# Fourier folds on one engine, half of their first level early, and other products between the folds and the DFT

## The chip, the core and the metric

The kernel runs on one core of a Trainium2 chip. The core has five engines that each work through a queue of their own in order: TensorE (PE in the profile, its weight loads PEld), VectorE (DVE), ScalarE (ACT), GpSimd (POOL) and SyncE (SP, which here only starts transfers). TensorE writes its products to eight PSUM banks; the other engines take them from there to SBUF. The metric is the device time of one execution in microseconds, the median of several runs.

## The reference

Two blocks follow each other, in float32. The first is a decayed linear attention over 4 batches, 8 heads, 768 positions and head size 64. Its output, as x of 4 x 768 x 512, goes through a Fourier mix, a normalisation and an MLP:

```
X = np.fft.fft(x, axis=1)
X = np.fft.fft(X, axis=2)
u = x + np.real(X)
un = (u - mean(u)) / sqrt(var(u) + 1e-6)
out = u + maximum(un @ w_ch1, 0) @ w_ch2        # w_ch1: 512 x 2048, w_ch2: 2048 x 512
```

The weights come as 64-bit floats, so the kernel turns them into float32 itself.

## The kernel before

**Stages of one batch.** `attn_chunk(b, c)` computes 128 of the 768 positions of batch b, for c from 0 to 5: transposes of k and q, scores, state, output and a last transpose into the tile x (for c of 3 and above: xn), which stays in SBUF and is also written to a tensor in DRAM, `xd[b]`. `fft_ln(b)` does the Fourier transform by symmetry. `mirror(b)` gathers rows of `xd[b]` in reversed order with indirect transfers that GpSimd issues: two tiles r0 and r1 (L339) and three tiles x (L342). `fold(b, r1)` adds and subtracts rows and columns that mirror each other, in two blocks of 128 and 65 rows (`BLK`). The even parts (tile e, L358, L359, L362, L368, L369, L375, L376) are VectorE's; the odd ones (tile o, L360, L361, L364, L371, L372, L378, L379) are GpSimd's. The results f and f1 (tag fs, fq) are the stationary operands of the sequence DFT (L395, five groups i, each over both blocks). `width` does the transform over columns (L406 to L411), lines 429 to 433 add the result to x, and three groups g of two tiles are normalised and transposed (L450 to L466). `mlp(b)` then goes through the three groups: 16 products with w1 (L477), whose results ScalarE and VectorE clip in turn (L483, L485), and two tiles T with 16 products with w2 each (L491), which VectorE adds to u and which are written out.

**Units of weights.** `weights()` converts the weights in 32 units (16 of w1, 16 of w2), each five instructions on VectorE (L216 to L224) and three on ScalarE.

**Order.** The kernel is written as generators that yield an estimate, in microseconds, of the TensorE work that they have just emitted. `weave(lead, other, ratio)` emits a step of `lead` and then steps of `other` until their sum is `ratio` times that of `lead`. When `other` runs out, the rest of `lead` is emitted in one go. The framework then fixes each engine's queue ahead of time: in the order of emission where the inputs are expected to be there, with later work moved ahead of what is expected to wait. At run time nothing overtakes.

- Batch 0's attention runs with 12 units of weights. Its `fft_ln(0)` runs beside half of batch 1's attention and 4 units.
- The rest of batch 1's attention and the start of `fft_ln(1)` run beside `mlp(0)` and the last 16 units.
- For batches 2 and 3, `front(b + 1)` (attention, then `fft_ln`) runs beside `mlp(b)` at the ratio 0.9 * t_mlp / t_front, 0.9 * 163.2 / 60.8 = 2.42.

**Rings.** Tiles of one tag share a ring of buffers. PSUM has a ring pa of five banks (attention, DFT, normalisation) and a ring pm of three (MLP). The tiles x come from a ring of ten, six of which a batch holds until its MLP tile T has been written.

Of the kernel before, what the change touches and what calls it, by code (L numbers as in the profile page):

```python
# [20 lines left out]
def _consts(B, S, DM):  # L21
# [38 lines left out]
    rows = [S // 2 - p, np.maximum(S // 2 - 128 - p, 0)]  # L60
    rev = [S - 128 * t - p for t in range(S // 256)]
    rows += [r % S for r in rev]
# [11 lines left out]
def kernel(  # L74
# [60 lines left out]
    z = fp.tile([H, 2 * C], F32, tag="fo", name="z")  # L135
# [28 lines left out]
    shifted = fp.tile([C, H, C], F32, tag="fe", name="shifted")  # L164
# [76 lines left out]
    def attn_chunk(b, c):  # L241
# [76 lines left out]
        if c == 0:  # L318
            xd[b] = dram.tile([S, DM], F32, name=f"xd{b}")
        nc.scalar.dma_start(xd[b][rows], x)  # L320
# [12 lines left out]
    def mirror(b):  # L333

        d = xd[b]
        gather = nc.gpsimd.indirect_dma_start
        r1 = [new(fp, [128, DM], f"r{a}") for a in range(2)]
        for a, n in enumerate(BLK):
            gather(out=r1[a][0:n], out_offset=None, in_=d[:, :], in_offset=row_of(a, n))  # L339
        for t in range(HC):  # L340
            u = xs[b, HC + t] = new(xp, [128, DM], "x")
            gather(out=u[:, :], out_offset=None, in_=d[:, :], in_offset=row_of(2 + t))  # L342
        for t in range(HC):
            xs[b, t] = xn_.pop((b, t))
        return r1

    def fold(b, r1):

        sets, odd = [], []
        for a, n in enumerate(BLK):  # L350
            x0, x2, x3 = xs[b, a][0:n], xn_[b, HC + a][0:n], xs[b, HC + a][0:n]
            x1 = r1[a][0:n]

            e, o = new(fp, [128, 2, 2 * W], "fe"), new(fp, [128, 2, 2 * W], "fo")
            f = new(fp, [128, 4, 2, QM], "fs", bufs=2)
            f1 = new(fp, [128, 2, 1], "fq", bufs=2)
            V, P = nc.vector, nc.gpsimd
            V.tensor_tensor(e[0:n, 0, 0:DM], x0, x3, op=ALU.add)  # L358
            V.tensor_tensor(e[0:n, 1, 0:DM], x1, x2, op=ALU.add)  # L359
            P.tensor_tensor(o[0:n, 0, 0:DM], x0, x3, op=ALU.subtract)  # L360
            P.tensor_tensor(o[0:n, 1, 0:DM], x1, x2, op=ALU.subtract)  # L361
            V.tensor_tensor(e[0:n, :, 1:HM], e[0:n, :, 1:HM], e[0:n, :, HM:DM - 1], op=ALU.add)  # L362
            nc.scalar.copy(e[0:n, :, HM:HM + 1], e[0:n, :, DM - 1:DM])
            P.tensor_tensor(o[0:n, :, 1:HM], o[0:n, :, 1:HM], o[0:n, :, HM:DM - 1], op=ALU.subtract)  # L364
# [19 lines left out]
    def fft_ln(b):  # L384
# [31 lines left out]
        def halves(t):  # L416
            return t.rearrange("p (r k) -> p r k", r=2)
# [170 lines left out]
```

## Time and profile before

| | |
|---|---|
| median of three runs | 1000.22 us (999.79 to 1003.56) |
| the profiled execution | 1007.08 us, its span 1005.3 us |
| mean granted TensorE clock | 0.937 of 2.4 GHz |
| TensorE busy | 892.6 us |
| VectorE, ScalarE, GpSimd busy | 323.7, 186.1 and 165.7 us |

All times inside the profile are of that one execution, from its first instruction. "Idle before" an instruction is the time in which its engine did nothing, put down to the event that ended it. The granted clock is a share of 2.4 GHz; 0.50 is 1.2 GHz.

### The profile page before, as it was taken

What the parts mean: (1) busy time and instruction counts of PE and PEld (TensorE: products, weight loads), DVE (VectorE), ACT (ScalarE), POOL (GpSimd) and SP (SyncE); (2) the same over time, 40 slices, a digit from 0 to 9 for tenths busy, and PEclk for the clock granted to TensorE, in tenths of its full rate; (3) what the DMA queues carried; (4) which work ended last, traced back from release to release, by engine and by line L of the source; (5) the groups of instructions that cost most, each with busy time, mean ns of one, the idle gap of its engine ahead of it and who ended that gap; (6) DMA issues with size and microseconds to landing.
All of it is one profiled execution on the core that took longest, in us unless ns stands there. A gap on an engine that the chain in (4) does not pass through costs nothing.

```text
span 1005.3 us, 10721 instructions
## 1 busy us (share of the span) xinstructions
PE 892.6 (89%) x4404; PEld 616.0 (61%) x4404; DVE 323.7 (32%) x610; ACT 186.1 (19%) x411; POOL 165.7 (16%) x176
## 2 busy tenths in 40 slices
PE   4642989598899999999986999999986999999997
PEld 3531867445575848658645848658646847576673
DVE  5978389833510101111124511111124411000100
ACT  4662247411010101111101101111101100000000
POOL 2219130413200001000034201000034200000000
PEclk9985799786999999999996999999995999999999
DMA  9982258400000002122120002121020000000000
GB/s 253 252 221 68 64 154 233 143 5 16 22 1 22 0 11 53 42 70 58 42 78 11 1 12 53 43 60 46 11 69 11 1 11 11 11 10 1 22 0 22
DMA packets 89265, 55.59 MB, mean 55 GB/s; under 512 B 76764, under 2 KB 78308, under 8 KB 89216
## 3 DMA queue, kind: packets, MB, share of 16 engines
q1 hardware_dynamic: 83264, 40.73, 15.5%
q0 software_dynamic: 2496, 7.87, 2.4%
q10 hardware_dynamic: 3456, 6.29, 1.7%
q8 instruction: 35, 0.57, 0.2%
q14 instruction: 14, 0.11, 0.0%
HBM read 42.29 MB, written 12.59 MB: 55 GB/s over the span
## 4 chain that ended last, share of the span: by engine, by line
PE 73%; POOL 6%; DVE 6%; issue 3%; DMA 3%; ACT 1%; POOLq 0%; ACTq 0%
PE pm L477 30%; PE pm L491 29%; PE pa L395 4%; PE pa L306 2%; PE pa L274 2%; DMA x<-xd,ix 1%; PE pa L302 1%; PE pa L465 1%; PE pa L313 1%; PE pa L289 1%; POOL fo L360 1%; POOL fo L364 1%; POOL r L339 1%; DVE pw L219 1%; PE pa L261 1%
## 5 line engine op out<-in xcount | busy, mean ns | idle before, releaser
L477 PE MATMUL pm<-ut,w 128*128 128x256 f32 x1536 | 356.9, 389 | 1.7 <-DVE hr L483 0.7
L491 PE MATMUL pm<-w,hr 128*128 128x512 f32 x768 | 338.5, 594 | 0.0
L477 PEld LDWEIGHTS pm<-ut,w 128*128 128x128 f32 x1536 | 293.3, 194 | 47.7 <-issue 5.4
L491 PEld LDWEIGHTS pm<-w,hr 128*128 128x128 f32 x768 | 143.3, 191 | 163.2 <-issue 162.2
L483 DVE TENSOR_SCALAR hr<-pm 128x256 f32<-128x256 f32 x96 | 40.6, 423 | 236.9 <-PE pm L477 236.9
L485 ACT ACTIVATE hr<-pm 128x256 f32<-128x256 f32 x96 | 36.6, 383 | 384.1 <-PE pm L477 379.9
L395 PE MATMUL pa<-cs,fs 65*128 65x193 f32 (+1 forms) x128 | 42.7, 509 | 63.8 <-DVE fs L375 49.6
L497 DVE TENSOR_TENSOR y<-pm,x 128x256 f32<-128x256 f32 x24 | 10.2, 424 | 218.6 <-PE pm L491 218.6
L395 PEld LDWEIGHTS pa<-cs,fs 65*128 65x128 f32 (+1 forms) x128 | 36.2, 309 | 70.1 <-issue 39.4
L502 POOL DMA_INDIRECT out_dram<-y,ix x12 | 12.5, 1043 | 325.2 <-DVE y L498 324.9
L252 POOL TENSOR_TENSOR kd<-k,decay 128x512 f32<-128x512 f32 x20 | 22.4, 1119 | 229.4 <-issue 136.1
L274 PE MATMUL pa<-qT,kT 64*128 64x128 f32 x384 | 30.5, 298 | 11.4 <-ACT qT L263 11.4
L278 DVE TENSOR_TENSOR sc<-pa,decay 128x512 f32<-128x512 f32 x48 | 31.3, 684 | 22.0 <-PE pa L274 20.3
L274 PEld LDWEIGHTS pa<-qT,kT 64*128 64x128 f32 x384 | 25.4, 199 | 21.0 <-ACT qT L263 14.1
L306 PE MATMUL pa<-sc,v 128*64 128x128 f32 x384 | 31.0, 291 | 5.7 <-DVE sc L278 5.7
L266 DVE TENSOR_TENSOR qs<-pa,qpow 128x512 f32<-128x512 f32 x20 | 13.8, 689 | 64.5 <-ACT qT L263 64.5
L306 PEld LDWEIGHTS pa<-sc,v 128*64 128x64 f32 x384 | 23.2, 143 | 12.6 <-DVE sc L278 8.2
L433 POOL TENSOR_TENSOR x<-x,ds 128x512 f32<-128x512 f32 x12 | 18.2, 1515 | 77.3 <-DVE ds L430 70.4
L339 POOL DMA_INDIRECT r<-xd,ix x8 | 8.6, 1079 | 129.4 <-DMA xd<-xn 128.2
L258 ACT COPY kT<-pa 128x512 f32<-128x512 f32 x24 | 14.1, 589 | 76.7 <-PE pa L256 76.6
L217 ACT ACTIVATE pw<-pw,cvt 128x512 uint16<-128x512 uint16 x32 | 22.9, 720 | 26.0 <-DVE pw L216 25.8
L309 ACT COPY oT<-pa 128x512 f32<-128x512 f32 x24 | 14.0, 585 | 65.0 <-PE pa L306 65.0
(94 smaller groups left out, 714.1 us busy)
## 6 DMA issues: line engine op xcount, KB each, us to landing
raw<-in_moe_w_ch_dram SPq DMA_DIRECT2D x32, 512.0 KB, 5.5
k<-in_k_dram SPq DMA_DIRECT2D x24, 256.0 KB, 3.3
q<-in_q_dram SPq DMA_DIRECT2D x24, 256.0 KB, 4.1
v<-in_v_dram SPq DMA_DIRECT2D x24, 256.0 KB, 3.4
xd<-x ACTq DMA_DIRECT2D x12, 256.0 KB, 2.7
xd<-xn ACTq DMA_DIRECT2D x12, 256.0 KB, 2.1
out_dram<-y SPq DMA_DIRECT2D x12, 256.0 KB, 2.0
cs<-k_cs SPq DMA_DIRECT2D x1, 772.0 KB, 6.9
```

Source lines behind the costliest of these rows:

```text
L217: nc.scalar.activation(pw, pw, AF.Relu, bias=cvt[:, 0:1], scale=-1.0)
L252: nc.gpsimd.tensor_tensor(kd, kt, kpow, op=ALU.mult)
L274: mm(pss[hi][:, hp, :], lhsT=kT[HD[hi], hp, :], rhs=qT[HD[hi], hp, :], start=True, stop=True)
L278: nc.vector.tensor_tensor(t, pss[hi], decay[:, hi::2, :], op=ALU.mult)
L306: mm(po[HD[hi], hp, :], lhsT=vt[:, 2 * hp + hi, :], rhs=sc[hi][:, hp, :], start=(c == 0 and hp == 0), stop=(hp == HP - 1), skip_group_chec ...
L339: gather(out=r1[a][0:n], out_offset=None, in_=d[:, :], in_offset=row_of(a, n))
L395: nc.tensor.matmul(ps[0:m, n, :], lhsT=f, rhs=cs[0:rows, a, i in (2, 3), n, :], start=(a == 0), stop=(a == 1))
L433: nc.gpsimd.tensor_tensor(halves(v_), halves(v_), halves(ds[:, 1:DM + 1])[:, ::-1, :], op=ALU.add)
L477: nc.tensor.matmul(ps, lhsT=w1[:, c, 128 * fc:128 * fc + 128], rhs=ut[:, c, :], start=(c == 0), stop=(c == KO - 1))
L483: nc.vector.tensor_scalar(t, ps, 0.0, None, op0=ALU.max)
L485: nc.scalar.activation(t, ps, AF.Relu)
L491: nc.tensor.matmul(ps, lhsT=hr[fc // 4][:, fc % 4, 128 * i:128 * i + 128], rhs=w2[:, fc, :], start=(fc == 0), stop=(fc == FO - 1))
```

## The change

1. All folds are VectorE's. Results overwrite parts of e and o instead of going to f and f1, and DFT groups read them there through `piece`.
2. `xd[b]` becomes two tensors: one for positions 128 to 639, one for 512 to 767 and row 0. Chunk 4 is written to both; of chunk 0 only one row is written.
3. `mirror_a(b)` is emitted at the end of chunk 4: it gathers r0, r1 and one tile x and does half of the first level of both blocks (`fold_x` with i = 1). `fold(b)`, after chunk 5, gathers the other two tiles x and does the rest. Tiles e and o now exist twice (fe0, fe1, fo0, fo1). What was one instruction on both halves of a block (L362, L364) is now one on each half.
4. `fft_ln` yields 7.0 after the folds, and 1.0 ahead of the transposes of each group g. t_front becomes 70.7, so that the ratio of batches 2 and 3 becomes 2.08.
5. For batch 0, `next(mix)` emits the folds. Then 0.3 t_att of batch 1's attention (two chunks) and two units of weights are emitted, then the DFT beside two further chunks and four units.
6. The addition of line 433 goes from GpSimd to VectorE.

```
@@ -57,9 +57,11 @@
     p = np.arange(128)
-    rows = [S // 2 - p, np.maximum(S // 2 - 128 - p, 0)]
+    ha, hb = S - 256, 128 * (S // 256) + 128
     rev = [S - 128 * t - p for t in range(S // 256)]
-    rows += [r % S for r in rev]
+    rows = [S // 2 - 128 - p, np.maximum(S // 2 - 256 - p, 0)]
+    rows += [r - hb for r in rev[:2]] + [r - 128 for r in rev[2:]]
     for b in range(B):
         rows += [S * b + np.where(r == S, S // 2, r) for r in rev]
     ix = np.ascontiguousarray(np.stack(rows, axis=1)).astype(np.uint32)
...
@@ -316,8 +318,14 @@
         nc.scalar.copy(x[:, 0:HM], px[:, 0:HM])
         nc.scalar.copy(x[:, HM:DM], px[:, DM - 1:HM - 1:-1])
         if c == 0:
-            xd[b] = dram.tile([S, DM], F32, name=f"xd{b}")
-        nc.scalar.dma_start(xd[b][rows], x)
+            xd[b] = (dram.tile([S - 256, DM], F32, name=f"xa{b}"), dram.tile([257, DM], F32, name=f"xb{b}"))
+            nc.scalar.dma_start(xd[b][1][256:257], x[0:1])
+        elif c < NC - 1:
+            nc.scalar.dma_start(xd[b][0][(c - 1) * C:c * C], x)
+        if c >= NC - 2:
+            nc.scalar.dma_start(xd[b][1][(c - NC + 2) * C:(c - NC + 3) * C], x)
+        if c == NC - 2:
+            mirror_a(b)
         yield 1.7
...
@@ -330,60 +338,73 @@
     for t in ys + bs:
         nc.gpsimd.memset(t, 0.0)
-    def mirror(b):
-        d = xd[b]
-        gather = nc.gpsimd.indirect_dma_start
+    gather = nc.gpsimd.indirect_dma_start
+    eo = {}
+    def fold_x(b, a, n, i, lo, hi):
+        e, o = eo[b][a]
+        tt = nc.vector.tensor_tensor
+        tt(e[0:n, i, 0:DM], lo, hi, op=ALU.add)
+        tt(o[0:n, i, 0:DM], lo, hi, op=ALU.subtract)
+        tt(e[0:n, i, 1:HM], e[0:n, i, 1:HM], e[0:n, i, HM:DM - 1], op=ALU.add)
+        tt(o[0:n, i, 1:HM], o[0:n, i, 1:HM], o[0:n, i, HM:DM - 1], op=ALU.subtract)
+    def mirror_a(b):
+        xa = xd[b][0]
         r1 = [new(fp, [128, DM], f"r{a}") for a in range(2)]
+        eo[b] = [(new(fp, [128, 2, 2 * W], f"fe{a}"), new(fp, [128, 2, 2 * W], f"fo{a}")) for a in range(2)]
         for a, n in enumerate(BLK):
-            gather(out=r1[a][0:n], out_offset=None, in_=d[:, :], in_offset=row_of(a, n))
-        for t in range(HC):
+            gather(out=r1[a][0:n], out_offset=None, in_=xa[:, :], in_offset=row_of(a, n))
+        for t in range(2, HC):
             u = xs[b, HC + t] = new(xp, [128, DM], "x")
-            gather(out=u[:, :], out_offset=None, in_=d[:, :], in_offset=row_of(2 + t))
+            gather(out=u[:, :], out_offset=None, in_=xa[:, :], in_offset=row_of(2 + t))
+        for a, n in enumerate(BLK):
+            fold_x(b, a, n, 1, r1[a][0:n], xn_[b, HC + a][0:n])
+    def fold(b):
+        for t in range(2):
+            u = xs[b, HC + t] = new(xp, [128, DM], "x")
+            gather(out=u[:, :], out_offset=None, in_=xd[b][1][:, :], in_offset=row_of(2 + t))
         for t in range(HC):
             xs[b, t] = xn_.pop((b, t))
-        return r1
-    def fold(b, r1):
-        sets, odd = [], []
+        sets = []
+        tt = nc.vector.tensor_tensor
         for a, n in enumerate(BLK):
-            x0, x2, x3 = xs[b, a][0:n], xn_[b, HC + a][0:n], xs[b, HC + a][0:n]
-            x1 = r1[a][0:n]
-            e, o = new(fp, [128, 2, 2 * W], "fe"), new(fp, [128, 2, 2 * W], "fo")
-            f = new(fp, [128, 4, 2, QM], "fs", bufs=2)
-            f1 = new(fp, [128, 2, 1], "fq", bufs=2)
-            V, P = nc.vector, nc.gpsimd
-            V.tensor_tensor(e[0:n, 0, 0:DM], x0, x3, op=ALU.add)
-            V.tensor_tensor(e[0:n, 1, 0:DM], x1, x2, op=ALU.add)
-            P.tensor_tensor(o[0:n, 0, 0:DM], x0, x3, op=ALU.subtract)
-            P.tensor_tensor(o[0:n, 1, 0:DM], x1, x2, op=ALU.subtract)
-            V.tensor_tensor(e[0:n, :, 1:HM], e[0:n, :, 1:HM], e[0:n, :, HM:DM - 1], op=ALU.add)
+            fold_x(b, a, n, 0, xs[b, a][0:n], xs[b, HC + a][0:n])
+            e, o = eo[b][a]
             nc.scalar.copy(e[0:n, :, HM:HM + 1], e[0:n, :, DM - 1:DM])
-            P.tensor_tensor(o[0:n, :, 1:HM], o[0:n, :, 1:HM], o[0:n, :, HM:DM - 1], op=ALU.subtract)
             am, bm = e[0:n, :, W:2 * W], o[0:n, :, W:2 * W]
             lo, hi = e[0:n, 0, 0:HM + 1], e[0:n, 1, 0:HM + 1]
-            V.tensor_tensor(am[:, 0, 0:HM + 1], lo, hi, op=ALU.add)
-            V.tensor_tensor(am[:, 1, 0:HM + 1], lo, hi, op=ALU.subtract)
+            tt(am[:, 0, 0:HM + 1], lo, hi, op=ALU.add)
+            tt(am[:, 1, 0:HM + 1], lo, hi, op=ALU.subtract)
+            lo, hi = am[:, :, 0:QM], am[:, :, HM:QM:-1]
+            tt(e[0:n, :, 0:QM], lo, hi, op=ALU.add)
+            tt(e[0:n, :, QM:HM], lo, hi, op=ALU.subtract)
             lo, hi = o[0:n, 0, 1:HM], o[0:n, 1, 1:HM]
-            P.tensor_tensor(bm[:, 0, 1:HM], lo, hi, op=ALU.subtract)
-            P.tensor_tensor(bm[:, 1, 1:HM], lo, hi, op=ALU.add)
-            lo, hi = am[:, :, 0:QM], am[:, :, HM:QM:-1]
-            V.tensor_tensor(f[0:n, 0], lo, hi, op=ALU.add)
-            V.tensor_tensor(f[0:n, 1], lo, hi, op=ALU.subtract)
+            tt(bm[:, 0, 1:HM], lo, hi, op=ALU.subtract)
+            tt(bm[:, 1, 1:HM], lo, hi, op=ALU.add)
             lo, hi = bm[:, :, 1:QM + 1], bm[:, :, HM - 1:QM - 1:-1]
-            P.tensor_tensor(f[0:n, 2], lo, hi, op=ALU.subtract)
-            P.tensor_tensor(f[0:n, 3], lo, hi, op=ALU.add)
-            nc.scalar.copy(f1[0:n], am[:, :, QM:QM + 1])
-            sets.append((f, f1))
-        return sets
+            tt(o[0:n, :, 0:QM], lo, hi, op=ALU.subtract)
+            tt(o[0:n, :, QM:HM], lo, hi, op=ALU.add)
+            sets.append((e, o))
+        eo.pop(b)
+        def piece(a, i, n):
+            c0 = W + QM if i == 4 else QM * (i % 2)
+            return sets[a][i in (2, 3)][0:BLK[a], n, c0:c0 + (1 if i == 4 else QM)]
+        return piece
     def fft_ln(b):
-        r1 = mirror(b)
-        sets = fold(b, r1)
+        piece = fold(b)
+        yield 7.0
         for i in range(5):
...
@@ -391,8 +412,7 @@
             m = 128 if i < 4 else 1
             for n in range(2):
                 for a, rows in enumerate(BLK):
-                    f = sets[a][0][0:rows, i, n, :] if i < 4 else sets[a][1][0:rows, n, :]
-                    nc.tensor.matmul(ps[0:m, n, :], lhsT=f, rhs=cs[0:rows, a, i in (2, 3), n, :],
+                    nc.tensor.matmul(ps[0:m, n, :], lhsT=piece(a, i, n), rhs=cs[0:rows, a, i in (2, 3), n, :],
                                      start=(a == 0), stop=(a == 1))
             nc.scalar.copy(ys[i][0:m, 0:2 * NK].rearrange("p (k n) -> p n k", n=2), ps[0:m])
             yield 1.4
...
@@ -430,7 +450,7 @@
             nc.vector.tensor_tensor(even_odd(ds[:, HM + 1:2 * HM + 1]), A, even_odd(B[:, :]), op=ALU.add)
             u, v_ = xs[b, t], xs[b, HC + t]
             nc.vector.tensor_tensor(halves(u), halves(u), halves(ds)[:, :, 0:HM], op=ALU.add)
-            nc.gpsimd.tensor_tensor(halves(v_), halves(v_), halves(ds[:, 1:DM + 1])[:, ::-1, :], op=ALU.add)
+            nc.vector.tensor_tensor(halves(v_), halves(v_), halves(ds[:, 1:DM + 1])[:, ::-1, :], op=ALU.add)
             yield 1.6
             if t == 0:
                 ps = psum_a([128, DM])
...
@@ -453,6 +473,7 @@
             rs = new(np_, [128, G], "rs")
             nc.gpsimd.tensor_scalar(ve, mv[:, :, 1], EPS, None, op0=ALU.add)
             nc.gpsimd.tensor_tensor(rs, ve, mhalf, op=ALU.pow)
+            yield 1.0
             ut = uts[b, g] = new(np_, [128, KO, G * 128], "ut")
             for i in range(G):
                 un = new(np_, [128, DM], "un", bufs=1)
...
@@ -540,16 +561,19 @@
     NW = KO * DFF // WP
     w = weights()
     t_mlp = NG * (FO * 1.7 + G * 4 * 3.4)
-    t_att, t_front = NC * 7.3, NC * 7.3 + 17.0
+    t_att, t_front = NC * 7.3, NC * 7.3 + 7.0 + 7.0 + 5.7 + 3 * 2.4
     run(weave(attn(0), part(w, 0.75 * NW), 0.75 * NW / t_att))
     fr = front(1)
-    run(weave(fft_ln(0), weave(part(fr, 0.5 * t_att), part(w, 0.25 * NW), 0.5 * NW / t_att), 1.5))
+    mix = fft_ln(0)
+    next(mix)
+    run(weave(part(fr, 0.3 * t_att), w, 0.1))
+    run(weave(mix, weave(part(fr, 0.3 * t_att), part(w, 0.25 * NW), 1.0), 1.0))
     for b in range(B):
         back = mlp(b)
         if b == 0:
-            run(weave(part(fr, 0.5 * t_att), weave(part(back, FO * 1.7 - 1.0), w, 0.9), 1.0))
+            run(weave(part(fr, 0.4 * t_att), weave(part(back, FO * 1.7 - 1.0), w, 0.9), 1.0))
             run(w)
             run(weave(fr, back, 1.0))
         elif b + 1 < B:
```

## Rows read from the trace of the kernel before

**Rows 1.** The page: busy us, share of the span and instructions of each engine.

```profile
PE 892.6 (89%) x4404; PEld 616.0 (61%) x4404; DVE 323.7 (32%) x610; ACT 186.1 (19%) x411; POOL 165.7 (16%) x176
```

**Rows 2.** Waits of PE, whole span: us in total, times, longest.

```profile
PE pa L395 <- DVE fs L375: 49.6, 4, 27.1
PE pa L395 <- POOL fs L378: 14.1, 3, 4.8
```

**Rows 3.** Busy us (instructions) by stretch: PE, PEld, DVE, ACT, POOL; PEclk, DMA, GB/s.

```profile
19.70:65.00 45.30, 30.41 (x400) 24.50 (x400) 42.05 (x70) 29.53 (x55) 10.04 (x10) 1.00 0.98 265
65.00:92.06 27.06, 0.01 (x2) 0.03 (x1) 18.87 (x22) 6.82 (x13) 16.65 (x15) 0.58 0.39 108
92.06:113.40 21.34, 17.95 (x85) 15.20 (x86) 10.71 (x16) 4.88 (x10) 9.26 (x7) 0.50 0.12 28
136.90:209.20 72.30, 56.43 (x366) 45.30 (x367) 63.03 (x118) 41.80 (x77) 18.39 (x18) 0.83 0.59 176
203.20:208.00 4.80, 4.49 (x11) 3.64 (x12) 4.80 (x10) 1.99 (x4) 0.00 (x0) 0.50 0.00 0
234.70:249.90 15.20, 15.15 (x50) 11.80 (x51) 1.39 (x4) 3.00 (x8) 1.17 (x2) 0.50 0.00 0
271.60:513.60 242.00, 242.00 (x1157) 163.79 (x1157) 32.49 (x69) 27.90 (x64) 10.70 (x12) 1.00 0.13 33
530.70:543.70 13.00, 8.17 (x22) 6.73 (x23) 8.91 (x9) 1.16 (x4) 9.56 (x9) 0.50 0.01 1
756.70:775.40 18.70, 13.82 (x39) 12.38 (x40) 8.95 (x10) 2.16 (x6) 9.61 (x9) 0.50 0.00 0
```

**Rows 4.** The same of line 224 alone, once for each weight unit: DVE busy.

```profile
136.90:209.20 72.30, 11.53 (x15) 0.83 0.59 176
```

**Rows 5.** Timeline around the third batch's fold: start, us, engine, line [idle before].

```profile
512.97 0.60 PE L313 MATMUL pa<-ident,oT 128*128 128x128 f32 x4
...
514.28 0.33 ACTq L320 DMA_DIRECT2D xd<-xn  x1
...
520.62 0.69 DVE L359 TENSOR_TENSOR fe<-r,xn 128x512 f32<-128x512 f32 x1 [15.80 <-DMA r<-xd,ix]
...
523.04 3.42 DVE L358 TENSOR_TENSOR fe<-x,x 128x512 f32<-128x512 f32 x1 [1.06 <-DMA x<-xd,ix]
523.40 1.28 POOL L361 TENSOR_TENSOR fo<-r,xn 128x512 f32<-128x512 f32 x1
...
530.71 2.52 PE L395 MATMUL pa<-cs,fs 128*128 128x193 f32 x6 [6.39 <-DVE fs L375]
...
539.76 2.30 PE L395 MATMUL pa<-cs,fs 65*128 65x193 f32 x6 [4.82 <-POOL fs L378]
```

**Rows 6.** Timeline around the first batch's fold.

```profile
65.72 0.33 ACTq L320 DMA_DIRECT2D xd<-xn  x1
...
77.35 0.69 DVE L359 TENSOR_TENSOR fe<-r,xn 128x512 f32<-128x512 f32 x1 [6.90 <-DMA r<-xd,ix]
...
92.06 0.98 PE L395 MATMUL pa<-cs,fs 128*128 128x193 f32 x2 [27.05 <-DVE fs L375]
...
98.24 0.41 DVE L369 TENSOR_TENSOR fe<-fe 65x257 f32<-65x257 f32 x1
```

**Rows 7.** Groups of instructions by line, shapes apart: busy, mean ns, idle before.

```profile
L358 DVE TENSOR_TENSOR fe<-x,x 128x512 f32<-128x512 f32 x4 | 10.7, 2687 | 4.3 <-DMA x<-xd,ix 4.3
...
L433 POOL TENSOR_TENSOR x<-x,ds 128x512 f32<-128x512 f32 x12 | 18.2, 1515 | 77.3 <-DVE ds L430 70.4 <-ACT ds L428 3.4 <-DMA x<-xd,ix 2.5
```

**Rows 8.** Waits of VectorE for a gather, whole span.

```profile
DVE fe L359 <- DMA r<-xd,ix: 37.7, 3, 15.8
```

**Rows 9.** Timeline around the second batch's late gather.

```profile
224.62 0.41 DVE L498 TENSOR_TENSOR y<-pm,x 128x256 f32<-128x256 f32 x1
...
225.31 0.98 POOL L342 DMA_INDIRECT x<-xd,ix  x1 [22.48 <-DVE y L498]
...
228.62 0.69 DVE L358 TENSOR_TENSOR fe<-x,x 65x512 f32<-65x512 f32 x1 [3.59 <-DMA x<-xd,ix]
```

More of the change, by code (lines that the diff above doesn't have):

```diff
@@ L130, in psum_m @@
         return new(pm, shape, "pm")
-    z = fp.tile([H, 2 * C], F32, tag="fo", name="z")
+    z = fp.tile([H, 2 * C], F32, tag="fo0", name="z")
     sq = const.tile([H, 8], F32, name="sq")
@@ L163 @@
     nc.vector.tensor_copy(flip, ident[:, ::-1])
-    shifted = fp.tile([C, H, C], F32, tag="fe", name="shifted")
+    shifted = fp.tile([C, H, C], F32, tag="fe0", name="shifted")
     nc.sync.dma_start(shifted, bass.AP(z0.tensor, z0.offset, [[1, C], [2 * C, H], [1, C]]))
```

## The prediction

> **What bounds the kernel now.** I read busy times first [rows 1]: TensorE works 892.6 of 1005.3 us, the others a third of the span or less. The kernel is bound by TensorE where TensorE is fed, as in the 242 us stretch without any idle time at full clock in [rows 3]. What can be won lies in the rest, so the waits of TensorE came next [rows 2]. Two of them, both of the DFT (L395) for the folds, make 49.6 + 14.1 = 63.7 us. Then I asked the stretches behind these waits for their granted clock [rows 3]: each of the four folds leaves TensorE at 0.50, that is at 1.2 instead of 2.4 GHz, for some time after work has resumed. Half of the busy time there is lost: 17.95/2 = 9.0 us behind batch 0's fold, (4.49 + 15.15)/2 = 9.8 behind batch 1's, 8.17/2 = 4.1 behind batch 2's and 13.82/2 = 6.9 behind batch 3's, together 29.8. All that the folds cost is so 63.7 + 29.8 = 93.5 us. More cannot be won by curing them alone.
>
> Last I read the timeline around a fold [rows 5] to see what the wait is made of. Batch 2: the last transpose ends at 513.57, and the first fold has its gathered rows at 520.62. That is 7.05 us for the copy of the tile, the write and the gather. TensorE's first DFT product starts at 530.71, the one that needs the 65-row block at 539.76: 10.1 and 19.1 us of folding. VectorE's L358 takes 3.42 us there, while L361 and its successor run on GpSimd; L359, of the same shape, takes 0.69 a little earlier, before GpSimd's folds begin. The mean of L358's 128-row form is 2.69 us [rows 7]. So the fold is slow because the two engines hold each other up, not because there is much to do.
>
> **What each part costs.** *All folds on VectorE.* Alone, a 512-wide fold takes 0.69 us [rows 5] and a 256-wide one 0.41 [rows 6]. A block now has 4 of the first and 12 of the second, 2.8 + 4.9 = 7.7 us, a batch 15.4 us. Half of the first level (2.2 us a block) is early. Behind the late gather 5.5 us a block are left, 11 us for both, where [rows 5] show 19.1. The bound from the other side is a loss: if the stretched durations came from something else than GpSimd's work, one engine with the work of two would need up to 2 x 19.1. I take 11, since 0.69 and 0.41 stand in the same program beside no fold of GpSimd's. Line 433 adds 12 x 0.69 = 8.3 us to VectorE, where GpSimd took 18.2 [rows 7]. In the MLP stretch VectorE is busy for 32.5 of 242 us [rows 3], so this hides there.
>
> *Early half.* Three of the five gathers move ahead of chunk 5. Behind them on GpSimd's queue stands nothing of chunk 5, which has no kd and no state. The written bytes stay as they were: one more write of 0.33 us on ScalarE's queue for chunk 4, one row instead of 128 for chunk 0. But the eight early folds enter VectorE's queue where they wait for the gather, ahead of chunk 5's qs and sc and of clipping (L483). VectorE already waits 37.7 us for gathered rows [rows 8], and TensorE did not stop for what stood behind, since the products with w2 need VectorE only once in four steps of 3.4. The early half is likely to meet products with w1, which want VectorE in every second step of 1.7; with three banks in pm the ring covers some 3.5 us. Between nothing and one such wait (7.05 less 3.5 us) in three batches, 0 to 10.6 us, I take 3, nearer to nothing, as VectorE's waits cost TensorE nothing so far.
>
> *Products between folds and DFT, batches 2 and 3.* Ratio 2.08 gives 14.5 us for the 7.0, and 3.5 for the last step of attention: 18 us of MLP behind the last transpose. The chain behind it is 7.05 + 1.5 for the second late gather + 5.5 for the second block, with the first block's folds in its shadow or just behind: 14 to 18 us. It just fits, with clipping and the additions of L497 in between. I leave 2 us of wait in each batch, below nothing to the 4.8 of today's second wait. For the clock I add nothing there: the shortest of the fold waits with 0.50 behind it is the 4.5 us of [rows 9]. Saved: 6.4 + 4.8 + 4.1 - 2 = 13.3 us in batch 2, and with 10.5 us of wait (63.7 less the 27.05, 10.52 + 4.50 and 6.39 + 4.82 of the others [rows 5, 6, 9]) 10.5 + 6.9 - 2 = 15.4 in batch 3.
>
> *Batch 0.* No MLP is there yet. TensorE stands still for 27.05 us from 65.0, of which the write and the gather take until 77.35, behind a stretch where transfers fill the queues to 0.98 [rows 3, 6]. Two chunks of batch 1's attention now go into the gap. A chunk takes 5.6 us of TensorE: 30.41 us in the first row of [rows 3], less 2.4 for the rest of chunk 0 (three of its seven groups of products are left there, an estimate by their number), by five chunks. Two are 11.2. The first block is folded at 77.35 + 5.5, about 83; the second at 88 or 89. TensorE so starts the DFT at about 84, having stood still for some 8 us, and waits some 2 us for the second block. The clock will still fall; I leave 4 of the 9 us. Saved: 27.05 + 9.0 - 10 - 4 = 22 us.
>
> *Batch 1 and the weights.* Sixteen units of weights are converted from 136.9 to 209.8 (15 in the window of [rows 4], one just behind it), 4.5 us each, with VectorE busy for 63.0 of 72.3 us [rows 3]. The change leaves 14 units for this stretch: 63 us. It begins 22 us earlier for the gap in batch 0, and some 6 later for the fourth chunk that now precedes it; so conversion ends at about 184 instead of 209, 25 us earlier. The first 10.5 us of batch 1's fold wait lie inside that stretch and save nothing more. The second wait, 4.5 us, and the slow clock behind it, 7.6, lie after it. They go, but for this: the ring of ten holds six tiles x of batch 0 and three of batch 1, and the early gather takes the tenth. Both late gathers need tiles that batch 0's MLP gives back with its first two outputs, where before this held for the second and third tile x: at 224.62 the output is added, at 228.62 the fold can start [rows 9]. The DFT of batch 1 therefore moves behind both outputs. Products with w1 of the next group can stand in for it; I leave 4 us. Saved 12.1 - 4 = 8. And TensorE, which has all it needs for w1 by then, can run half of the 13.6 us of products with w2 for its first output (four steps of 3.4) beside the conversion: 7 us. Saved in all 25 + 8 + 7 = 40; the 22 of batch 0 are in the 25.
>
> The Trainium skill speaks against moving work to VectorE here: Perfetto Trace Analysis, section Optimizing Scalar/DVE Operations, says that with VectorE saturated, giving some of its work to ScalarE or even to GpSimd may make sense. The same sentence adds that the two share a read port, so that it may not help. The stretched L358 bears out that second half; no row shows a saturated VectorE with GpSimd's folds away. By the first half alone the sum would be 19 us smaller (the second rival).
>
> **Sum.** 40 + 13.3 + 15.4 - 3 = 65.7 us. The profiled execution took 1007.08 us, so it would take 941.4. It is 6.9 us above the median of the runs shown; I carry this over and predict 934 us.
>
> **Rivals.** *The conversion is not VectorE's bound.* If in the first 270 us TensorE is also freed of batch 1's first wait (10.5 us and 2.2 of slow clock) and overlaps the other half of the first output (7 us), 20 us more go, 12.7 + 7: 914. For it speaks that VectorE is idle for 9 of 72 us there and that its folds become shorter; against it, that the units come one in 4.5 us now.
>
> *VectorE becomes the bound of the early stretch.* GpSimd's share of the folds, 2 x (3 x 0.69 + 4 x 0.41) = 7.4 us a batch, and 2.1 for line 433, come to VectorE in both of the first batches: 19 us, if nothing is given back. Then 953. For it speaks 63.0 of 72.3; against it, that stretched folds take as much VectorE time today as twice the number will alone.
>
> *The transfers set the end.* If write and gather become slower beside the products that are now moved in, as in batch 0 (12.35 us from 65.0 to 77.35, instead of 7.05), every fold ends some 5 us later and the clock falls each time: four times 5, 955.
>
> *VectorE blocks TensorE.* The folds stand in its queue ahead of qs, sc and clipping, and the queue is fixed ahead. If each early and each late wait stopped TensorE for its transfers and folds, less the 3.5 us that the ring covers, a batch would lose (7.05 + 4.4 - 3.5) + (7.05 + 11 - 3.5) = 22.5 us and some 7 us by the clock, four batches 118, where 3 are in the sum: 934 - 3 + 118 = 1049. It decides from a loss of 17 us a batch on (the 68.7 us that the other terms save, by four). Against it: the 15.8 us wait in [rows 5] cost TensorE nothing.
>
> *Nothing changes.* TensorE stands still for only 6.39 of the 17.1 us between the transpose and the DFT of [rows 5]: MLP products have been moved into the gap already. If the wait followed the DFT wherever it is emitted, and the shorter folds were eaten by the longer queue, it would stay at 1000. Against it: L358's 3.42 us.
>
> **Chances.** Forecast 0.50; 914: 0.16; 953: 0.17; 955: 0.08; blocked: 0.06; nothing: 0.03. What a measurement can tell from no change is about 0.5%, 5 us. Faster 0.91, same 0.03, slower 0.06. The range goes from 903, where nearly all of the 93.5 is won, to 966, where the second rival and half of the third come together (934 + 19 + 10) and the early folds cost 3 more: 0.9 of the cases lie in it by these numbers, less with the errors of their terms.
>
> **What would show it.** Right: L395's waits for VectorE under 20 us in all; folds of 0.69 and 0.41 us; no stretch at half clock behind the folds of batches 2 and 3; the last L224 at about 184. Wrong: L483 or sc (L278) as releasers of TensorE, long waits of VectorE for r or x with L477 behind, or units that end as late as today.

## The result

The changed kernel takes 958.12 us in the median (956.57 to 960.03, four runs); the kernel before took 1000.95 us beside it (999.79 to 1003.56). The ratio is 0.957, with a 95% interval of 0.9539 to 0.96. That is 42.8 us less, where the prediction had 66: inside the range, above the forecast of 934. The profiled execution took 959.64 us (span 957.3, mean granted clock 0.968), so that the two profiled executions lie 47.4 us apart.

Busy times on the page of the changed kernel, against [rows 1]. GpSimd's work has halved, VectorE's has become less although it now does all the folds:

```profile
PE 872.7 (91%) x4404; PEld 601.0 (63%) x4404; DVE 312.7 (33%) x694; ACT 184.9 (19%) x403; POOL 86.9 (9%) x108
```

TensorE's waits, against [rows 2] (us in total, times, longest). L415 is the DFT: its waits for folds went from 63.7 to 2.2 us. At the head stand the attention products L308, which wait for the masked scores sc, and L498, the products with w1:

```profile
PE pa L308 <- DVE sc L280: 30.6, 10, 16.7
PE pm L498 <- ACT hr L506: 11.1, 1, 11.1
...
PE pa L486 <- DVE un L482: 5.4, 1, 5.4
...
PE pa L415 <- DVE fe L387: 1.5, 1, 1.5
...
PE pa L415 <- DVE fe L383: 0.7, 1, 0.7
```

The folds of the third and fourth batch cost 8 and 14 us at half clock and 21.7 us of waits before [rows 2, 3, 5]. In the changed kernel they lie elsewhere in time, so that one long stretch with both of them is compared, first before, then changed (columns as in [rows 3]):

```profile
262.00:900.00 638.00, 613.98 (x2843) 421.36 (x2843) 135.54 (x266) 75.83 (x189) 82.29 (x86) 0.97 0.11 30
262.00:900.00 638.00, 636.36 (x2945) 429.42 (x2944) 136.40 (x322) 75.98 (x187) 41.62 (x53) 1.00 0.11 30
```

What TensorE still waits for behind 262 us is 1.6 us for scores and nothing for folds, at full clock. VectorE waits 15 us for rows at the third batch's late fold, and the DFT starts at 501.91 us without a wait, 17.0 us after the last transpose:

```profile
PE pa L308 <- DVE sc L280: 1.6, 3, 1.3
```

```profile
484.30 0.60 PE L315 MATMUL pa<-ident,oT 128*128 128x128 f32 x4
...
491.65 0.69 DVE L348 TENSOR_TENSOR fe<-x,x 128x512 f32<-128x512 f32 x1 [15.07 <-DMA x<-xb,ix]
```

The first 262 us are another matter. Before, in five stretches:

```profile
0.00:60.00 60.00, 34.99 (x392) 26.54 (x392) 47.49 (x92) 34.76 (x63) 13.99 (x26) 1.00 0.97 250
60.00:110.00 50.00, 17.99 (x108) 14.52 (x106) 34.58 (x46) 14.13 (x27) 25.91 (x21) 0.59 0.36 100
110.00:160.00 50.00, 44.76 (x411) 37.07 (x412) 35.57 (x76) 24.90 (x55) 13.03 (x16) 0.93 0.56 158
160.00:210.00 50.00, 34.93 (x187) 26.67 (x185) 44.01 (x76) 26.44 (x49) 14.12 (x12) 0.80 0.47 140
210.00:262.00 52.00, 46.54 (x143) 26.55 (x142) 17.81 (x38) 5.03 (x18) 13.52 (x13) 0.84 0.03 11
```

The same stretches of the changed kernel:

```profile
0.00:60.00 60.00, 37.26 (x365) 28.77 (x366) 43.55 (x87) 32.03 (x57) 12.42 (x25) 1.00 0.93 238
60.00:110.00 50.00, 24.22 (x222) 20.51 (x222) 39.19 (x81) 22.92 (x45) 15.84 (x10) 0.69 0.56 162
110.00:160.00 50.00, 40.94 (x353) 32.74 (x352) 32.99 (x73) 20.26 (x47) 7.97 (x11) 0.90 0.44 120
160.00:210.00 50.00, 32.81 (x154) 24.48 (x152) 34.86 (x70) 24.87 (x45) 3.03 (x3) 0.83 0.45 131
210.00:262.00 52.00, 49.81 (x200) 32.25 (x199) 20.95 (x53) 6.18 (x20) 4.12 (x4) 1.00 0.06 20
```

Busy time times granted clock is a rough measure of the work that TensorE has done. Up to 110 us the changed kernel is 8.4 us ahead (37.26 + 24.22 x 0.69 = 54.0 against 45.6), up to 210 us only 2.9 (118.1 against 115.2). It wins another 10.7 between 210 and 262 us. The same sum over slices of 1 us, in which the clock is no average over waits, gives 10.1 and 5.6 us for the first two. What it does in the gap of batch 0 is for a good part lost again within the next 100 us.

The timeline shows how. Start, duration, engine, instruction, and idle time before it with what ended it:

```profile
70.53 0.33 ACTq L326 DMA_DIRECT2D xb<-xn  x1
...
77.17 0.68 DVE L280 TENSOR_TENSOR sc<-pa,decay 128x512 f32<-128x512 f32 x1
...
77.91 0.69 PE L308 MATMUL pa<-sc,v 128*64 128x128 f32 x2 [4.59 <-DVE sc L280]
...
84.77 0.69 DVE L348 TENSOR_TENSOR fe<-x,x 128x512 f32<-128x512 f32 x1 [5.62 <-DMA x<-xb,ix]
...
94.52 0.68 DVE L280 TENSOR_TENSOR sc<-pa,decay 128x512 f32<-128x512 f32 x1
...
95.25 1.97 PE L308 MATMUL pa<-sc,v 128*64 128x128 f32 x14 [16.65 <-DVE sc L280]
...
106.92 0.33 PE L415 MATMUL pa<-cs,fe 128*128 128x193 f32 x1
```

Of the two score tiles of batch 1's first chunk, the second stands in VectorE's queue behind the late folds of batch 0. These wait for rows until 84.77; the scores come at 94.52, and TensorE stands still for 16.65 us, in products that were meant to fill the gap. Of these, 5.62 us are VectorE's wait for rows and 9.8 us the folds themselves, with one pass of the conversion among them. The DFT starts at 106.9, where it started at 92.06 in [rows 6]. In a second profile of the same kernel (the run of the changed kernel again, below) the long wait is 13.0 us and the DFT starts at 103.4. The conversion of the weights shares that queue; its last instruction (first and last start in this view) is at 200.3 us, where the prediction had 184 and the kernel before 209.8:

```profile
L226 DVE SCALAR_TENSOR_TENSOR w<-w,pw x32: 677/686/949, 13.2 to 200.3; 128x512 f32<-128x512 f32 x32
```

### The profile page after: what moved, and what is told of

Same layout as the page of the kernel before. It is cut to its first block, busy times and chain, and to the rows that moved or that the text cites. A ratio compares the mean times of both kernels' runs of the same rounds, so it can differ in the third digit from the quotient of the medians.

```text
span 957.3 us, 10694 instructions
## 1 busy us (share of the span) xinstructions
PE 872.7 (91%) x4404; PEld 601.0 (63%) x4404; DVE 312.7 (33%) x694; ACT 184.9 (19%) x403; POOL 86.9 (9%) x108
## 5 line engine op out<-in xcount | busy, mean ns | idle before, releaser
L498 PE MATMUL pm<-ut,w 128*128 128x256 f32 x1536 | 354.3, 386 | 12.4 <-ACT hr L506 11.1
L498 PEld LDWEIGHTS pm<-ut,w 128*128 128x128 f32 x1536 | 289.5, 192 | 57.4 <-ACT hr L506 11.5
L308 PE MATMUL pa<-sc,v 128*64 128x128 f32 x384 | 32.5, 295 | 30.7 <-DVE sc L280 30.6
L308 PEld LDWEIGHTS pa<-sc,v 128*64 128x64 f32 x384 | 24.1, 146 | 38.4 <-DVE sc L280 34.5
L280 DVE TENSOR_TENSOR sc<-pa,decay 128x512 f32<-128x512 f32 x48 | 31.3, 685 | 25.5 <-PE pa L276 23.8
L276 PE MATMUL pa<-qT,kT 64*128 64x128 f32 x384 | 30.6, 304 | 8.1 <-ACT qT L265 8.1
L276 PEld LDWEIGHTS pa<-qT,kT 64*128 64x128 f32 x384 | 25.7, 204 | 17.5 <-ACT qT L265 11.2
L482 DVE TENSOR_SCALAR un<-x,mv,rs 128x256 f32<-128x256 f32 x48 | 17.6, 408 | 23.1 <-PE pa L486 18.7
L304 PE MATMUL pa<-qs,st 64*64 64x128 f32 x320 | 23.9, 290 | 0.1
L221 DVE SCALAR_TENSOR_TENSOR pw<-raw,pw 128x512 uint16<-128x512 uint16 x32 | 22.9, 723 | 1.4 <-ACT pw L220 1.0
L225 DVE SCALAR_TENSOR_TENSOR w<-w,raw 128x512 f32<-128x512 uint32 x32 | 23.0, 722 | 0.7
```

The source lines that it names most:

```text
L221: nc.vector.scalar_tensor_tensor(pw, top, 0x8000, pw, op0=ALU.bitwise_and, op1=ALU.bitwise_or)
L225: nc.vector.scalar_tensor_tensor(dst, d, 2.0 ** -20, lof, op0=ALU.mult, op1=ALU.add)
L276: mm(pss[hi][:, hp, :], lhsT=kT[HD[hi], hp, :], rhs=qT[HD[hi], hp, :], start=True, stop=True)
L280: nc.vector.tensor_tensor(t, pss[hi], decay[:, hi::2, :], op=ALU.mult)
L304: mm(po[HD[hi], hp, :], lhsT=s_old[HD[hi], hp, :], rhs=qs[HD[hi], hp, :], start=(hp == 0), stop=False, skip_group_check=True)
L308: mm(po[HD[hi], hp, :], lhsT=vt[:, 2 * hp + hi, :], rhs=sc[hi][:, hp, :], start=(c == 0 and hp == 0), stop=(hp == HP - 1), skip_group_chec ...
```

## The experiments

Three groups of four kernels, each group on one chip with the kernel before, which took 1002.77, 1002.54 and 1004.81 us there; the groups ran on three chips. "Kernel" in an expectation is the changed one unless it says otherwise. Since the framework plans each queue anew for each kernel, a run differs from its neighbour in more than the lines of its diff; this is the limit of what they show.

**One engine alone.** The kernel before, with one line changed:

```
-            V, P = nc.vector, nc.gpsimd
+            V, P = nc.vector, nc.vector
```

> The kernel before with one edit: the odd folds go to VectorE too. No early half, nothing between folds and DFT. If the folds were slow because GpSimd and VectorE held each other up, a batch's folds take 15.4 us on VectorE instead of 19.1 and every fold of 512 takes about 0.69 us: the DFT of batches 2 and 3 waits some 3 to 5 us less each, the time falls by 10 to 25 us, to 976 to 991. If their length came from something else, they add up on one engine: L358 stays over 1 us and the time rises to 1010 or more.

Measured: 951.55 us (950.62 to 956.07), ratio 0.9508 (0.9436 to 0.9581). This line alone gives the whole gain, and at least as much as all parts together. It is at least twice what was expected, which counted batches 2 and 3 alone; the first 262 us gained as well. VectorE's L358 takes 0.69 us in the mean of its 128-row form (2.69 in [rows 7]), the products with w1 start at 125.1 instead of 136.9 us, and the conversion's last instruction at 192.1 instead of 209.8. Of TensorE's waits for folds 19.1 us are left at batch 0's DFT and 9.4 in four others:

```profile
PE pa L395 <- DVE fs L375: 28.5, 5, 19.1
```

**No early half.** The changed kernel, with `mirror_a(b)` emitted at the start of `fold(b)`:

```
-        if c == NC - 2:
-            mirror_a(b)
...
     def fold(b):
+        mirror_a(b)
```

> The changed kernel with the early half undone: all five gathers and all folds are emitted after chunk 5. If the early half is needed beside the products emitted in between, the chain behind the last transpose grows by 4.4 us of folds and two gathers, past the 18 us of products: DFT waits of 3 to 8 us in batches 2 and 3 and slow clock behind them, 8 to 20 us slower than the changed kernel (966 to 978). If the products in between are cover enough, the two stay within 4 us, or this one gains what the early folds cost in batch 1 (4.8 us of waiting for scores).

Measured: 948.97 us (947.37 to 950.18), ratio 0.9462 (0.9393 to 0.9531). That gains more than the second alternative allowed. L308's waits fall from 30.6 to 15.0 us; behind 262 us TensorE waits 1.1 us in all.

**No products between.** The changed kernel without its yields of 7.0 and 1.0, with the old t_front and with batch 0 woven as before:

```
-        yield 7.0
...
-    mix = fft_ln(0)
-    next(mix)
-    run(weave(part(fr, 0.3 * t_att), w, 0.1))
-    run(weave(mix, weave(part(fr, 0.3 * t_att), part(w, 0.25 * NW), 1.0), 1.0))
+    run(weave(fft_ln(0), weave(part(fr, 0.5 * t_att), part(w, 0.25 * NW), 0.5 * NW / t_att), 1.5))
```

> The changed kernel without anything emitted between folds and DFT: no yield of 7.0, the ratios and the start of batch 0 as in the kernel before. If emission order is what freed batches 2 and 3, waits of 5 to 8 us come back there, each with slow clock: 15 to 30 us slower than the changed kernel (973 to 988). If the shorter folds alone did it, batches 2 and 3 stay free of waits and the time is within 5 us of the changed kernel.

**Batch 0 alone as before.** The same, but the yields and t_front of batches 1 to 3 stay:

```
-        yield 7.0
+        if b:
+            yield 7.0
```

> The changed kernel with batch 0 emitted as in the kernel before (DFT groups straight behind the folds, half of batch 1's attention beside them), all else kept. My theory: in batch 0 the wait only moved, from the DFT to the scores (L280), which stand in VectorE's queue behind folds that wait for the late gather; so putting the old emission back costs little, 0 to 8 us (958 to 966), with the DFT waiting some 20 us in its place. The recorded forecast has 22 us there: then 975 or more. Rival: the conversion of weights bounds the early stretch whatever stands in batch 0's gap: then 958 within 3 us, and the last unit ends at the same time, about 201.

Measured: 949.9 us (949.43 to 950.38) and 950.02 us (949.67 to 952.54), ratios 0.9475 (0.9407 to 0.9544) and 0.9485 (0.9415 to 0.9555). Both lie below everything that was expected of them. They do not differ: in batches 1 to 3 the products between buy nothing that can be measured once the folds are one engine's. In the second of them batch 0's DFT waits again, and the scores wait less:

```profile
PE pa L416 <- DVE fe L387: 22.0, 2, 20.7
PE pa L308 <- DVE sc L280: 14.1, 12, 6.7
```

**The changed kernel again**, unedited, in the group of the next three.

> The changed kernel as it is, beside the next three on one chip. The kernels of the first four runs took 949 to 952 us where the kernel before took 1002.77. If the early half and the products between really cost 7 to 9 us (first theory), this one takes 956 to 961 us. If they cost nothing and the first comparison was made on a slower chip (rival), it takes 949 to 952.

Measured: 955.77 us (955.02 to 959.93), ratio 0.9536 (0.9492 to 0.958). The group of the first four had the same time for the kernel before (1002.77 and 1002.54), so that the early half seems to cost 6.8 us and batch 0's new order 5.8; the intervals of the ratios overlap, and the runs were not on one chip. TensorE's waits for scores are much as in the first profile:

```profile
PE pa L308 <- DVE sc L280: 31.2, 13, 13.0
```

**Batch 0's folds behind two chunks.** The two late gathers, now in a function `late`, stay where they are:

```
     def fft_ln(b):
-        piece = fold(b)
-        yield 7.0
+        late(b)
+        if b == 0:
+            yield 7.0
+        piece = fold(b)
+        if b:
+            yield 7.0
```

> The late gathers of batch 0 stay where they are; its late folds go into VectorE's queue behind two chunks of batch 1's attention instead of ahead of them. Theory one: the scores of these chunks stand behind folds that wait for a gather. Then TensorE's waits for scores of 4.6 and 16.7 us around 78 to 95 us go, the DFT of batch 0 starts at 90 to 95 instead of 106.8, and the time falls by 8 to 20 us, to 938 to 950. Theory two: the conversion of the weights sets the end of the first 200 us whatever stands before. Then the last unit still ends at 198 to 201, the wait goes to the products with w1, and the time falls by less than 5 us, to 953 or more.

Measured: 949.98 us (948.72 to 954.94), ratio 0.9479 (0.9432 to 0.9526). The long wait is gone, the one ahead of it is longer, and the DFT starts 10.7 us earlier than in the unedited kernel beside it (103.44 us) and 14 earlier than in the timeline above:

```profile
77.98 0.69 PE L308 MATMUL pa<-sc,v 128*64 128x128 f32 x2 [8.55 <-DVE sc L280]
79.88 1.97 PE L308 MATMUL pa<-sc,v 128*64 128x128 f32 x14 [1.21 <-DVE sc L280]
...
92.79 0.49 PE L422 MATMUL pa<-cs,fe 128*128 128x193 f32 x2
```

The conversion's last instruction comes at 189.1 instead of 196.4 in the unedited kernel beside it. That is 7.3 us earlier, and so are the products with w1, which start at 130.1 instead of 137.3. So the end of the conversion is not fixed by the units alone: what stands before them moves it.

**All folds behind the scores.** As in the last run; besides, `fold_x` of the early half is emitted in chunk 5, behind its scores, in every batch.

> As the run before, and in every batch the early folds go behind the scores of the sixth chunk instead of ahead of them. Theory one: the 4.8 us wait for scores at 176 us goes as well, and 3 to 6 us more are saved than in the run before, to 933 to 946. Theory two: no more than 2 us between the two runs, since TensorE then waits for the weights instead.

Measured: 945.75 us (944.03 to 953.91), ratio 0.9452 (0.9395 to 0.951); the conversion's last instruction is at 186.6. The wait around 176 us is gone; the 4.2 us between this run and the last one are within what the executions of each differ by.

**Gathers early, no fold early.** As the run with batch 0's folds behind two chunks, and the early `fold_x` is done in `fold(b)`:

```
-        for a, n in enumerate(BLK):
-            fold_x(b, a, n, 1, r1[a][0:n], xn_[b, HC + a][0:n])
+        xr[b] = r1
...
+            fold_x(b, a, n, 1, xr[b][a][0:n], xn_[b, HC + a][0:n])
             fold_x(b, a, n, 0, xs[b, a][0:n], xs[b, HC + a][0:n])
```

> Gathers as in the changed kernel, early ones included, but no fold is early: every fold stands behind the late gathers, and in batch 0 all of them stand behind two chunks of batch 1's attention. Theory one, scores stand behind folds that wait for rows: VectorE's 10.7 us of waits for the early gather go, TensorE's waits for scores fall under 10 us after 60 us, and the time is 938 to 946. Theory two, VectorE's work in the conversion is what counts in any order: no change of place gives more than the 945.75 of the run with all folds behind the scores, so 945 to 952.

Measured: 941.83 us (941.14 to 945.13), ratio 0.9391 (0.9351 to 0.9431), faster than the kernel before and the changed one, and the lowest median of those that do the whole computation. Not all went as expected. TensorE's waits for scores behind 60 us are 11.0 us, not under 10, and VectorE's waits for the early gather are still 12.0: the framework puts batch 0's first folds ahead of a score again, behind which TensorE waits 9.4 us. The stretch behind 60 us, against its two rows above:

```profile
60.00:110.00 50.00, 34.78 (x322) 28.68 (x322) 42.48 (x85) 26.17 (x52) 13.52 (x11) 0.83 0.61 165
```

**Units without three passes of VectorE.** The lines of `load_weights` that make sign and exponent are left out (three of VectorE's five passes, two of ScalarE's three).

> A unit of weights leaves out the conversion's sign and exponent: three of VectorE's five passes and two of ScalarE's three, so that the weights are not those of the reference; the loads, the folds and their order stay. Theory two, the conversion sets the end of the early stretch: the last unit ends by 180 instead of 200.9, the 11.1 us wait for ScalarE's clipping goes, and 15 us or more are saved, 943 or less. Theory one, the scores behind the folds: the waits for scores stay at over 20 us in all, since their gathers come no earlier, and less than 10 us are saved, 948 or more.

**Units without two passes of ScalarE**, with all five of VectorE's kept:

```
-        nc.scalar.activation(pw, pw, AF.Relu, bias=cvt[:, 0:1], scale=-1.0)
-        nc.scalar.activation(pw, pw, AF.Relu, bias=cvt[:, 1:2], scale=-8.0)
```

> A unit of weights leaves out two of ScalarE's three passes, those that turn the exponent, so that the weights are not the reference's; all five passes of VectorE stay. If VectorE's passes set the pace of the conversion, as the 25.8 us saved by leaving out three of them (1.8 us in each of 14 units) suggest, this saves less than 8 us: 948 or more. If the handing over between ScalarE and VectorE sets it, most of those 25.8 us are saved here too: 940 or less.

Measured: 930.01 us (928.12 to 931.51) without VectorE's three, 955.79 us (952.93 to 958.07) without ScalarE's two, against 955.77 for the kernel as it is. Since the first of these two runs leaves out ScalarE's two passes as well, it is the second, in another group, that tells them apart: without ScalarE's two nothing is saved, without VectorE's three besides 25.8 us. In the first the last unit is done by 171.6 us, 25.5 earlier than in the unedited kernel beside it:

```profile
L218 DVE SCALAR_TENSOR_TENSOR w<-w,raw x32: 676/688/1542, 11.4 to 170.9; 128x512 f32<-128x512 uint32 x32
```

Not all of this comes from the last 14 units, as three passes of 0.41, 0.68 and 0.68 us in each of them (24.8 us) might suggest: the products with w1 already start 12.3 us earlier, at 125.0 instead of 137.3, and the other 13.2 us are won behind that. So VectorE's passes set the pace, and ScalarE's two do not. The prediction of the other theory, waits for scores of over 20 us, missed too: they fell to 10.3. Units and folds stand ahead of the scores in one queue; taking units away shortens the waits as moving folds does.

**Odd folds back on GpSimd**, in the order of the changed kernel (`fold_x` and the second level alike):

```
-        tt(o[0:n, i, 0:DM], lo, hi, op=ALU.subtract)
+        nc.gpsimd.tensor_tensor(o[0:n, i, 0:DM], lo, hi, op=ALU.subtract)
```

> The changed kernel with the odd folds given back to GpSimd; order, early half and products between stay. Theory one, the two engines hold each other up: folds of the late half take 1 to 3.4 us again instead of 0.42 to 0.69, TensorE waits for folds or for scores by 20 us more, and the time rises by 15 to 40 us, to 971 to 996. Rival, the gain came from the order of emission: with two engines the folds are no slower, and the time stays within 5 us of the 955.77 that the changed kernel took.

Measured: 967.86 us (965.8 to 971.33), ratio 0.964 (0.9594 to 0.9685), 10 to 12 us above the changed kernel: less than the 15 to 40 expected, more than the rival's 5. The folds are slow again. Groups of instructions by line and shape (busy, mean ns) with GpSimd:

```profile
L350 DVE TENSOR_TENSOR fe<-fe 65x255 f32<-65x255 f32 x8 | 11.9, 1492 | 0.1
...
L348 DVE TENSOR_TENSOR fe<-r,xn 65x512 f32<-65x512 f32 x4 | 4.8, 1188 | 1.7 <-DMA r<-xa,ix 1.7
```

and in the changed kernel:

```profile
L350 DVE TENSOR_TENSOR fe<-fe 65x255 f32<-65x255 f32 x8 | 3.3, 414 | 0.0
...
L348 DVE TENSOR_TENSOR fe<-r,xn 65x512 f32<-65x512 f32 x4 | 2.7, 683 | 0.0
```

But behind 262 us TensorE waits no longer for them: 2.6 us in all, none of it for folds. What is lost lies in batch 1, where its DFT waits 6.7 us for folds, 4.0 of them for one of GpSimd's, and the stretch from 210 to 262 us falls back to the clock that it had before the change:

```profile
PE pa L415 <- POOL fo L393: 4.0, 1, 4.0
```

```profile
210.00:262.00 52.00, 45.30 (x143) 27.77 (x142) 14.53 (x22) 4.16 (x13) 13.64 (x14) 0.84 0.06 20
```

**One addition back on GpSimd** (L453, twelve instructions, `nc.vector` to `nc.gpsimd`).

> The changed kernel with one of the two additions after the DFT given back to GpSimd, twelve instructions. The prediction puts their 8.3 us on VectorE where they hide behind products of the MLP: then the time stays within 5 us of 955.77. If VectorE's queue is short of time in the first 200 us (six of the twelve lie there), the run is 2 to 5 us faster; if GpSimd's 1.5 us instruction holds VectorE up, it is slower by up to 6.

Measured: 963.17 us (959.49 to 963.42), ratio 0.9581 (0.954 to 0.9622). The addition takes 1.54 us there instead of 0.68, and VectorE's own addition beside it 0.75 instead of 0.70. The time is 5 to 7 us above the changed kernel's two medians, but in another group, and the intervals of the ratios overlap: it is not faster, whether it is slower stays open.

## Why the prediction was in the range, and what was wrong in it

| term, us | forecast | measured |
|---|---|---|
| batch 0, conversion, products with w2, less 3 for the early folds | 25 + 7 - 3 = 29 | 2.9 (work done by 210 us; 5.6 in slices of 1 us) |
| batch 1's second wait and its slow clock | 8 | 10.7 (210 to 262 us) |
| batches 2 and 3 | 13.3 + 15.4 = 28.7 | 32.7 |
| sum | 65.7 | 46.3 (the spans differ by 48.0) |

The 32.7 are the waits of 6.39, 4.82 and 10.5 us and the 4.1 and 6.9 us of slow clock that the prediction took from before: nothing of either is left. The measured time is in the range, but the sum was too large by a third, and one of its terms came to a tenth or a fifth of its size. The upper end of the range, 966, which the result needed, was built from rivals whose causes the runs bear out in part at most; to that extent it was luck.

**Right: folds of 0.69 and 0.41 us.** They take 0.68 to 0.69 and 0.41 to 0.43, and with GpSimd back beside them up to 1.19 and 1.49 in the mean. That VectorE's own folds slow down beside GpSimd's is so shown from both sides, by giving the odd folds to VectorE in the old kernel (51 us saved) and by taking them back in the new one (10 to 12 lost). No run parts this from GpSimd's being slower at its own folds, which goes away with them; but of the 63.7 us of waits for folds in [rows 2], 49.6 end with a fold of VectorE's. The Trainium skill, Perfetto Trace Analysis, section Optimizing Scalar/DVE Operations, says that offloading some work of a saturated VectorE to GpSimd may make sense, and in the sentence after that GpSimd and VectorE share a read port, so that it might not help. The runs side with the warning: neither the odd folds (0.73 to 2.23 us each in the means by shape) nor the addition (1.54 us) became cheaper on GpSimd.

**Wrong in its reason: "It just fits" in batches 2 and 3.** The chain came out as forecast, 17.0 us in the third batch where the prediction had 14 to 18, and left no wait. But the prediction needed both faster folds and 18 us of products between, and each alone is almost enough. One engine without products between leaves two waits there, 1.5 us together (3.4 in the run with one line changed); the rest of the change with the slow folds of two engines leaves none for folds. They are two cures of one stall and do not add up: 51 us for one engine alone, some 37 for the rest of the change with two engines (1004.81 less 967.86), 43 to 47 for both.

**The step that failed: batch 0.** "TensorE so starts the DFT at about 84, having stood still for some 8 us ... Saved 22." The prediction put two chunks of attention into the gap by their TensorE time, 11.2 us, and did not ask where the scores of these chunks stand in VectorE's queue. They stood behind folds that wait for rows, and behind these folds' own 9.8 us. The wait did not go; it moved from the DFT to L308, as 4.59 + 16.65 us (7.2 + 13.0 in the second profile), and the DFT started at 106.9 or 103.4 instead of 84. In the first profile the last write was also issued late, at 70.53, 4.8 us later than in [rows 6]; in the second it came at 66.70, so that this is no part of the cause. This is the mechanism of the rival "VectorE blocks TensorE", which the prediction knew and priced for every batch or none. It came in batch 0 and, with 4.78 us at 176 us, in batch 1, where no MLP work stands ready; in batches 2 and 3 the 15 us waits of VectorE for rows cost nothing. Putting batch 0's folds behind the scores won 5.8 us in the medians, the early folds behind theirs another 4.2, both on one chip; only the first is clear of what the executions of one kernel differ by. By work done in slices of 1 us, the run with one line changed is 16.2 us ahead of the kernel before at 210 us and the one with no fold early 19.5, where the changed kernel is 5.6 ahead.

**The conversion.** "Conversion ends at about 184 instead of 209" rested on that step: units that start 22 us earlier. The last units run with the products with w1. These were to start at 136.9 - 22 + 6, about 121 us, and started at 140.8 (137.3 in the second profile):

```profile
140.78 1.22 PE L498 MATMUL pm<-ut,w 128*128 128x256 f32 x2 [0.68 <-ACT ut L487]
```

From there the 14 units took 60 us, to 200.9, where the prediction had 63: the pace of 4.5 us each was nearly right, and the start was missed by 20 us. The 11.1 us wait of L498 lies in this stretch: the clipping of its results stands in ScalarE's queue among the passes of the units. That VectorE sets this pace was right: three passes fewer saved 25.8 us, two of ScalarE's none. So the rival by which the conversion is not VectorE's bound falls. The rival that VectorE becomes the bound of the early stretch was near in size (953). VectorE's queue does set the time there, as the lighter units show; but its cause, the work added to VectorE, is not what the runs show: the odd folds alone on VectorE saved 51 us, another order with the same work took 14 us less than the changed kernel, and taking 8.3 us of additions from VectorE did not help. The early half, put at 3 us, seems to cost some 7. Slower transfers (955) are no cause in the third batch: from the end of the last transpose to the fold it takes 6.8 us there, where [rows 5] have 7.05. In batch 0 the way from the last write to the late fold is 14.2 us (13.1 in the second profile), against 11.6 to the first fold in [rows 6], a small part of what was missed.

**The base.** Both profiled executions lie above their medians, by 6.1 us before and by 1.5 after. Carrying the first over to the forecast (6.9 us) made it lower by some 5 us than it would be with the 1.5 of the result.

**Open.** How much of the difference between 958 and 942 us is the early folds' place and how much the new plan of the queues; how much of what GpSimd's folds cost is their own length and how much VectorE's slowing down; and whether the addition on GpSimd costs time.

## What to carry to other kernels

When products are moved into a gap, follow each of them through every queue that it needs: filler whose own scores stand behind the late work on another engine only moves the wait. Before adding cover for a slow chain, try what the chain takes without the contention; here one line did as much as the whole change. Start transfers early, but emit the work that waits for them behind the work that is ready.

## What was not expected of the hardware

A fold of 65 x 255 takes VectorE 0.41 us alone and 1.49 us in the mean beside GpSimd's folds, more than three times as long; two engines with half of the folds each were slower than one with all. And two passes of ScalarE in each of 32 units, some 0.7 us each or 45 us together, could be left out without a change in the time (955.79 against 955.77 us), while three of VectorE's left out besides, 1.8 us a unit, were worth 25.8 us.
